# Chunk 0 of a fused attention and FFN kernel: the value projection before q and k, with x and wv loaded side by side

## The chip, the cores and the metric

The kernel runs on one NeuronCore of a Trainium2 chip. The metric is the device time of one execution in microseconds (us), lower is better. Six runs of the kernel before gave a median of 273.89 us, from 273.71 to 274.6.

The core has a matrix engine (TensorE, PE in the profile; its weight loads are PEld), which multiplies a stationary and a moving operand from the on-chip memory SBUF and writes to eight accumulator banks (PSUM); a vector engine (VectorE, DVE), a scalar engine (ScalarE, ACT), GpSimd (POOL), and SyncE (SP). DMA transfers are started by an instruction on SP's or ACT's queue and carried by 16 DMA engines. Engines run on their own and wait for each other on semaphores. Each engine takes its instructions in order.

## What is computed

An input x of 2048 tokens by 512 goes through two branches, which a gate mixes token by token:

```
g = sigmoid((x * gate_w).sum(-1))
a = A(x)                       # attention in 4 segments with a carried memory
b = (relu_gate * up) @ W_down  # FFN: gate = x @ W_gate, up = x @ W_up, F = 1792
out = g * a + (1 - g) * b
```

In A there are 32 heads of 16. q, k and v are x @ wq, x @ wk and x @ wv (512 x 512 each). For each segment of 512 tokens, causal softmax attention within the segment is mixed with a read of a memory matrix M, built from phi(k) and v of the segments before; then comes a projection with wo. All tensors are bf16.

## The kernel before

The kernel is written for four chunks of 512 tokens (NSEG = 4), each of them a segment of the attention. For each chunk there are the projections (`proj`), scores, exponentials and the product with v (`att`, L666), the memory update (`mu`) and its read (`nd`), the FFN (`ffn`, L739), and the output projection (`outp`, L763). A matmul has up to 512 columns; a projection of one chunk is 16 matmuls of 128x512 for each of q, k and v: four output tiles with four contraction tiles (kt) each. q and k come out transposed, four tiles of 128 features by 512 tokens (L581, weights stationary); v comes out by tokens, four tiles of 128 tokens by 512 features (L579, x stationary). So a tile of q or k needs x of all 512 tokens, and a tile of v needs x of its own 128 tokens and all four tiles of wv.

**Who sets the order.** `program` does not write instructions directly. It makes operations (`Op`) that name their engine, an assumed cost and the resources they read and write, and puts them into queues with a priority for each engine (`sc.queue`). A planner (`Sched.run`) then simulates the engines: whenever an engine is free, it takes the head of the queue with the best priority among the heads that are ready by its cost model, and adds the semaphore waits that the resources ask for. The result is a fixed order of instructions for each engine. One queue's operations never overtake each other. TensorE's queues are, by priority: the start (`xps`, 0) and scores (0), memory (1), projections (2), gate matmuls and output (3), FFN (4). An accumulator bank is taken by an `Epoch` when its first matmul is planned, and comes free when its readers are planned; the class "proj" may hold two at once by the planner's account. The planner assumes that DMAs move 340 bytes per ns one after another and land 1.7 us later at the start of the kernel.

**The start.** Loads of 128 KB each go out on two queues (L416 to L421). SP has x row tiles 0 and 2 (into the buffer hT), wq tiles 0 and 2, wk 0 to 3, wv 0 to 3, then beta, the FFN weights wg and wu in halves, the transposed x of chunk 1, gwb, wo and wd (L435 to L441). ACT has x tiles 1 and 3, wq 1 and 3, and gate_w (g4, 1 KB). DVE clears a 128x128 buffer (L473) and the four accumulators. TensorE then works through `xps`: five matmuls of 512 columns on the cleared buffer (`warm(5, 0, 3)`, L482), whose result nobody reads; for each of the four x tiles, four matmuls with the identity, which transpose it into one PSUM bank (L490); and four more of the unread matmuls (`warm(4, 1, 0)`). DVE copies the transposed tiles 0 and 2 to xT, ACT tiles 1 and 3 (L496, L498), 512 columns each. Then the projections begin: q0 and q1 alternate by contraction tile, one matmul for each semaphore wait (L574, L610), then q2, q3, k0 to k3 and v0 to v3 in steps of two matmuls (L609). DVE copies each finished tile out (L588, L594, L607), and masks k per head parity (`kmask`, L597); score matmuls (L679) follow when the first of these is done, exponentials on ACT (L684). The gate's small matmuls (L514, L527) turn gate_w and need g4.

`xt(0)` names the resources of chunk 0's transposed x, one for each row tile; every projection matmul of chunk 0 waits for all four.

The softmax here doesn't subtract the row's maximum and nothing guards it: scores larger than these inputs give would overflow.

## Time and profile before

| | us |
|---|---|
| median of six runs | 273.89 |
| lowest and highest | 273.71, 274.6 |
| the profiled execution | 274.6 |
| its span, first to last instruction | 272.8 |
| TensorE busy in the span | 267.7 |
| VectorE, ScalarE, GpSimd busy | 206.0, 192.8, 123.2 |
| first transposing matmul (L490) starts | 3.29 |
| first projection matmul (L581) starts | 6.99 |

The profile follows one execution. It lists every instruction with its start and duration by engine, and groups them by source line. A duration of a matmul is from its start to the end of its way through the array, and such durations overlap: matmuls in a row start closer together than they last. For a wait it names the instruction or transfer that ended it. "The chain" follows the last instruction back, at each step to what released it. A DMA has the time of its issue, which is an instruction on a queue, and of its landing, when the last of its 16 completion counts arrives; a busy share or a rate of DMA is over all 16 engines. In views by stretches, columns are time busy on each engine with the number of instructions, TensorE's granted clock, DMA share and GB/s.

### The profile page before, as it was taken

What the parts mean: (1) busy time and instruction counts of PE and PEld (TensorE: products, weight loads), DVE (VectorE), ACT (ScalarE), POOL (GpSimd) and SP (SyncE); (2) the same over time, 40 slices, a digit from 0 to 9 for tenths busy, and PEclk for the clock granted to TensorE, in tenths of its full rate; (3) what the DMA queues carried; (4) which work ended last, traced back from release to release, by engine and by line L of the source; (5) the groups of instructions that cost most, each with busy time, mean ns of one, the idle gap of its engine ahead of it and who ended that gap; (6) DMA issues with size and microseconds to landing.
All of it is one profiled execution on the core that took longest, in us unless ns stands there. A gap on an engine that the chain in (4) does not pass through costs nothing.

```text
span 272.8 us, 5368 instructions
## 1 busy us (share of the span) xinstructions
PE 267.7 (98%) x2156; PEld 115.0 (42%) x2156; DVE 206.0 (76%) x421; ACT 192.8 (71%) x182; POOL 123.2 (45%) x171
## 2 busy tenths in 40 slices
PE   6999999999999999999999999999999999999996
PEld 3444434344434544344344444344444343444445
DVE  5689989999989998999978949596774256787200
ACT  3289887788696877889578769985866768782122
POOL 4013566628585676847385663242233343331000
PEclk9999999999999999999999999999999999999999
DMA  6999654011001323120112111000111100000011
GB/s 226 304 348 251 199 87 102 13 40 41 20 2 40 79 58 79 38 48 13 22 38 61 38 42 35 21 2 0 23 37 22 38 23 19 0 2 1 0 41 38
DMA packets 31026, 17.01 MB, mean 62 GB/s; under 512 B 20761, under 2 KB 31001, under 8 KB 31001
## 3 DMA queue, kind: packets, MB, share of 16 engines
q1 hardware_dynamic: 30416, 16.14, 23.3%
q10 hardware_dynamic: 584, 0.53, 0.6%
q8 instruction: 17, 0.28, 0.4%
q14 instruction: 9, 0.07, 0.1%
HBM read 9.84 MB, written 2.10 MB: 44 GB/s over the span
## 4 chain that ended last, share of the span: by engine, by line
PE 93%; DVE 3%; DMA 2%; ACT 1%; issue 0%; SPq 0%; DVEq 0%
PE psA L749 36%; PE psA L788 18%; PE psA L581 10%; PE psL L679 9%; PE psA L704 7%; PE psA L579 5%; PE psA L781 5%; DMA wq<-in_A_wq_dram 2%; PE psA L654 1%; PE psA L625 1%; DVE gexpT L546 1%; ACT E L684 1%; PE psA L641 1%; DVE hT L760 1%; SPq L414 0%
## 5 line engine op out<-in xcount | busy, mean ns | idle before, releaser
L684 ACT ACTIVATE E<-psL 128x2048 bf16<-128x2048 f32 x80 | 150.0, 1875 | 39.4 <-PE psL L679 38.8
L687 POOL TENSOR_SCALAR_AFFINE_SELECT E<-E 128x512 bf16<-128x512 bf16 x128 | 83.1, 667 | 116.3 <-ACT E L684 113.3
L749 PE MATMUL psA<-xT,wu 128*128 128x512 bf16 x224 | 59.8, 380 | 0.0
L749 PE MATMUL psA<-xT,wg 128*128 128x512 bf16 x224 | 59.5, 380 | 0.1
L788 PE MATMUL psA<-wd,hT 128*128 128x512 bf16 (+1 forms) x238 | 54.6, 367 | 0.0
L760 DVE TENSOR_TENSOR hT<-psA,rl 128x512 bf16<-128x512 f32 x56 | 38.3, 683 | 14.0 <-PE psA L749 13.1
L788 PEld LDWEIGHTS psA<-wd,hT 128*128 128x128 bf16 x238 | 21.7, 98 | 24.3 <-issue 3.7
L597 POOL TENSOR_SCALAR kp<-kT,pm 128x512 bf16<-128x512 bf16 x19 | 30.7, 1620 | 2.6 <-PE psL L679 1.2
L679 PE MATMUL psL<-qT,kp 32*128 32x384 bf16 (+3 forms) x512 | 31.7, 301 | 0.0
L749 PEld LDWEIGHTS psA<-xT,wu 128*128 128x128 bf16 x224 | 20.4, 98 | 25.4 <-issue 3.3
L749 PEld LDWEIGHTS psA<-xT,wg 128*128 128x128 bf16 x224 | 20.0, 98 | 24.6 <-issue 3.7
L709 DVE STREAM_TRANSPOSE Tn<-psA 128x512 f32<-128x512 f32 x32 | 21.5, 697 | 8.0 <-PE psA L704 7.9
L757 ACT ACTIVATE rl<-psA 128x512 bf16<-128x512 f32 x28 | 16.7, 597 | 12.7 <-PE psA L749 12.5
L679 PEld LDWEIGHTS psL<-qT,kp 32*128 32x128 bf16 x512 | 8.9, 92 | 31.7 <-ACT E L684 14.4
L758 DVE TENSOR_SCALAR rl<-psA 128x512 bf16<-128x512 f32 x28 | 19.0, 680 | 3.6 <-PE psA L749 2.9
L704 PE MATMUL psA<-E,vaug 128*17 128x256 bf16 (+3 forms) x512 | 21.1, 300 | 0.0
L581 PE MATMUL psA<-xT,wq 128*128 128x512 bf16 x64 | 16.5, 380 | 1.3 <-DMA wq<-in_A_wq_dram 1.3
L781 PE MATMUL psA<-wo,oT 128*128 128x512 bf16 (+1 forms) x68 | 16.5, 367 | 0.0
L581 PE MATMUL psA<-xT,wk 128*128 128x512 bf16 x64 | 16.4, 381 | 0.0
L797 DVE TENSOR_SCALAR osb<-psA,omg 128x512 bf16<-128x512 f32 x8 | 6.0, 746 | 12.9 <-PE psA L788 12.9
L579 PE MATMUL psA<-wv,xT 128*128 128x512 bf16 x64 | 15.7, 380 | 0.0
L798 ACT ACTIVATE osb<-psA,omg 128x512 bf16<-128x512 f32 (+1 forms) x9 | 5.8, 639 | 13.7 <-PE psA L781 13.3
(75 smaller groups left out, 235.6 us busy)
## 6 DMA issues: line engine op xcount, KB each, us to landing
out_dram<-osb SPq DMA_DIRECT2D x15, 128.0 KB, 1.7
wg<-in_B_W_gate_dram SPq DMA_DIRECT2D x8, 224.0 KB, 5.2
wu<-in_B_W_up_dram SPq DMA_DIRECT2D x8, 224.0 KB, 5.8
wd<-in_B_W_down_dram SPq DMA_DIRECT2D x1, 1792.0 KB
osb<-in_A_x_dram SPq DMA_DIRECT2D x12, 128.0 KB, 2.2
wk<-in_A_wk_dram SPq DMA_DIRECT2D x4, 128.0 KB, 5.2
wv<-in_A_wv_dram SPq DMA_DIRECT2D x4, 128.0 KB, 4.7
wo<-in_A_wo_dram SPq DMA_DIRECT2D x1, 512.0 KB, 5.3
```

The lines of the kernel that those rows point to most:

```text
L579: ins = e.matmul(A(ep)[:, :], lhsT=V.xT[:, kt, tok + col * 128:tok + (col + 1) * 128], rhs=w[:, kt, :], start=(kt == 0), stop=(kt == KT - 1))
L581: ins = e.matmul(A(ep)[:, :], lhsT=w[:, kt, col * 128:(col + 1) * 128], rhs=V.xT[:, kt, tok:tok + 512], start=(kt == 0), stop=(kt == KT - 1))
L597: km = lambda e, G=G, p=p, ks=ks: e.tensor_scalar(V.kp[:, ks, :], V.kT[:, G, :], V.pm[:, p:p + 1], None, ALU.mult)
L679: ins = q.matmul(PL[:, jj, o:o + w], lhsT=V.kp[32 * jj:32 * jj + 32, kslot(s, n), 128 * j:128 * j + 128], rhs=V.qT[32 * jj:32 * jj + 32, q ...
L684: acts.append(act(lambda a, e=e: a.activation(V.E[:, e, :, :], PL[:, :, :], ACT.Exp, scale=SCALE), t_act(2048), reads=[f"bankL{b}" for b i ...
L687: pools.append(pool(lambda g, ap=ap: g.affine_select(out=ap, in_=ap, compare_op=ALU.is_ge, fill=0.0, base=0, pattern=[[0, 4], [1, 128]], c ...
L704: ins = q.matmul(A(ep)[32 * jj:32 * jj + 17, c:512], lhsT=V.vaug[:, s % 2, j, 8 * G + 2 * jj + p, :], rhs=V.E[:, e, jj, o:o + w], start=(j ...
L709: ds.append(dve(lambda e, p=p, ep=eps[p]: e.transpose(V.Tn[:, p, :], A(ep)[:, :]), t_dve(512), writes=[f"Tn{p}"], name=f"tr{s}_{G}_{p}", e ...
L749: ins = e.matmul(A(ep)[:, :], lhsT=w[:, kt, f * 128:(f + 1) * 128], rhs=V.xT[:, kt, c * 512:(c + 1) * 512], start=(kt == 0), stop=(kt == K ...
L760: evs.append(dve(lambda e, ep=eu, r=r, hs=hs: e.tensor_tensor(V.hT[:, hs, :], A(ep)[:, :], V.rl[:, r, :], ALU.mult), t_dve(512), reads=[f" ...
L781: ins = e.matmul(A(ep)[:, 0:c1 - c0], lhsT=V.oT[:, o0 + G, i * 128:(i + 1) * 128], rhs=V.wo[:, G, c0:c1], start=st_ and G == 0, stop=sp_ a ...
L788: ins = e.matmul(A(ep)[:, 0:c1 - c0], lhsT=V.hT[:, slots[f], i * 128:(i + 1) * 128], rhs=V.wd[:, f, c0:c1], start=st_ and f == f0, stop=sp ...
```

## The change

The new order of loads pairs each x row tile on SP with the wv tile of the same number on ACT. wq, wk and gate_w follow on SP alone.

The transposes of each x tile are split into two halves of two matmuls, each with a PSUM bank of its own (eight halves take turns in four banks). DVE copies the first half of every tile to xT and ACT the second, 256 columns each, and there is one resource for each half.

The value projection of chunk 0 moves into TensorE's start queue. Its matmuls wait for the wv tiles they use and, alone among the projections, only for the half of the x tile they use. q and k of chunk 0 follow in the order q0, k0, q1, k1 and so on, all in steps of two matmuls; the alternation of q0 and q1 is gone.

The unread matmuls at the start read a constant that the program start writes, in place of the buffer that DVE cleared; there are six instead of five, and the four after the transposes are gone.

```diff
 def xt(c):
-    return [f"xT{c}_{kt}" for kt in range(KT)] if c else [f"xT0_{i}" for i in range(4)]
+    return [f"xT{c}_{kt}" for kt in range(KT)] if c else [f"xT0_{i}_{h}" for i in range(4) for h in range(2)]
...
-for i, eng in enumerate(("sp", "act", "sp", "act")):
-    load(eng, [f"hT{i}"], V.hT[:, i, :], x0[:, i, :], 1 << 17)
-for nm, w, src in (("wq", V.wq, A_wq), ("wk", V.wk, A_wk), ("wv", V.wv, A_wv)):
+for i in range(4):
+    load("sp", [f"hT{i}"], V.hT[:, i, :], x0[:, i, :], 1 << 17)
+    load("act", [f"wv{i}"], V.wv[:, i, :], A_wv[i * 128:(i + 1) * 128, :], 1 << 17)
+for nm, w, src in (("wq", V.wq, A_wq), ("wk", V.wk, A_wk)):
     for kt in range(KT):
-        load("act" if nm == "wq" and kt % 2 else "sp", [f"{nm}{kt}"], w[:, kt, :], src[kt * 128:(kt + 1) * 128, :], 1 << 17)
-load("act", ["g4"], V.g4[:], gate_w.rearrange("(kt p) -> kt p", p=128), 1 << 12)
+        load("sp", [f"{nm}{kt}"], w[:, kt, :], src[kt * 128:(kt + 1) * 128, :], 1 << 17)
+load("sp", ["g4"], V.g4[:], gate_w.rearrange("(kt p) -> kt p", p=128), 1 << 12)
...
-ds.append(dve(lambda e: e.memset(V.rl[:, 0, 0:128], 0.0), 130, writes=["rl0"], name="warm0"))
...
-            ins = e.matmul(PL[:, b, :], lhsT=V.rl[:, 0, 0:128], rhs=V.rl[:, 0, 0:128].unsqueeze(1).to_broadcast([128, 4, 128]), start=True, stop=True)
+            ins = e.matmul(PL[:, b, :], lhsT=nc.const_aps.tensor(1.0, [128, 128], BF16), rhs=nc.const_aps.tensor(1.0, [128, 512], BF16), start=True, stop=True)
...
-xps, xcs = [warm(5, 0, 3)], []
+xps, xcs = [warm(6, 0, 3)], []
 for i in range(4):
...
+    for h in range(2):
+        bk = (2 * i + h) % 4
...
+            for k in range(2):
+                kt = 2 * h + k
+                ins = e.matmul(PL[:, bk, k * 128:(k + 1) * 128], lhsT=V.hT[:, i, kt * 128:(kt + 1) * 128], rhs=V.ident[:], start=True, stop=True)
...
+        if h == 0:
+            xcs.append(dve(lambda e, d=dst, s_=srcp: e.tensor_copy(d, s_), t_dve(256), reads=[f"bankL{bk}"], writes=[f"xT0_{i}_{h}"], name=f"xc{i}_{h}"))
+        else:
+            xcs.append(act(lambda e, d=dst, s_=srcp: e.activation(d, s_, ACT.Copy), t_act(256), reads=[f"bankL{bk}"], writes=[f"xT0_{i}_{h}"], name=f"xc{i}_{h}"))
-xps.append(warm(4, 1, 0))
-sc.queue(0, xps)
...
-        step = 1 if s == 0 and name == "q" and col < 2 else 2
+        step = 2
...
-            pes.append(pe(fn, mm(512, step), reads=[f"{wname}{kt}" for kt in range(k0, k0 + step)] + xt(s), ...
+            pes.append(pe(fn, mm(512, step), reads=[f"{wname}{kt}" for kt in range(k0, k0 + step)] + ([f"xT0_{col}_{k0 // 2}"] if s == 0 and tokmajor else xt(s)), ...
...
     if s == 0:
-        pes = [p for k in "qkv" for p in pes if p.name[0] == k]
-        pes[:2 * KT] = [pes[h * KT + kt] for kt in range(KT) for h in range(2)]
+        vs = [p for p in pes if p.name[0] == "v"]
+        pes = [p for p in pes if p.name[0] != "v"]
+        sc.queue(0, xps[:5] + vs[0:1] + xps[5:7] + vs[1:2] + xps[7:] + vs[2:])
```

In the last line, `xps` holds the unread matmuls, then the halves of row tiles 0 to 3 in order, and `vs` the two halves of v0, v1, v2 and v3.

## The prediction

> **What bounds the kernel now.** I read the page first, for the share of each engine and the chain that ended last; then the busy time by stretches of the span; then TensorE's timeline and the chain within the first 20 us; then the DMA issues one by one and the bytes moved in those microseconds.

> ```profile
> PE 267.7 (98%) x2156; PEld 115.0 (42%) x2156; DVE 206.0 (76%) x421; ACT 192.8 (71%) x182; POOL 123.2 (45%) x171
> ...
> PE 93%; DVE 3%; DMA 2%; ACT 1%; issue 0%; SPq 0%; DVEq 0%
> ```

> TensorE is busy 98% of the span and is 93% of the chain. The stretches show where the other 5.1 us are:

> ```profile
> core 0: us, PE busy (x) PEld busy (x) DVE busy (x) ACT busy (x) POOL busy (x), PEclk, DMA share, GB/s
> ...
> 4.28:7.69 3.41, 2.15 (x17) 1.02 (x15) 1.04 (x2) 1.40 (x3) 0.19 (x1) 1.00 1.04 348
> ...
> 11.10:18.30 7.20, 7.20 (x43) 2.96 (x42) 6.63 (x18) 4.37 (x6) 0.65 (x1) 1.00 1.04 385
> 18.30:260.00 241.70, 241.37 (x2008) 101.81 (x2007) 193.66 (x393) 182.64 (x167) 119.15 (x155) 1.00 0.20 46
> ```

> Between 18.3 and 260 us TensorE misses 0.33 us in all. So nothing downstream can absorb or win back a shift: if the projections of chunk 0 end a microsecond earlier or later, so does the kernel. Only the first 18 us need a sum. TensorE's own timeline there:

> ```profile
> 1.04 2.31 PE L482 MATMUL psL<-rl 128*128 128x512 bf16 x5 [1.04 <-DVE rl L473]
> 3.29 1.52 PE L490 MATMUL psL<-ident,hT 128*128 128x128 bf16 x16
> 4.69 1.04 PE L482 MATMUL psL<-rl 128*128 128x512 bf16 x4
> 6.99 1.89 PE L581 MATMUL psA<-xT,wq 128*128 128x512 bf16 x8 [1.26 <-DMA wq<-in_A_wq_dram]
> ```

> L482 computes nothing that is used. Useful are the 16 transposes (L490) and, from 6.99 on, 48 projection matmuls in a row (16 each of q, k, v), with nothing missing between them. The 6.99 is set by a transfer, as the chain says:

> ```profile
> 1.71 5.19 DMA wq<-in_A_wq_dram
> 6.89 0.09 issue
> 6.99 1.89 PE psA L581 x8
> ```

> **Units.** Eight q matmuls take 1.89 us, the last one 0.38 long: (1.89 - 0.38) / 7 = 0.216 us apart. The last six transposes start 0.056 apart. Before: 6.99 + 48 x 0.216 = 17.36 us for the end of the projections (a gate matmul of 0.11 and the first score matmuls come on top in both kernels).

> **When the data is there.** Each queue issues a 128 KB load about every 0.47 us, so the first eight go out as four pairs, one on SP and one on ACT. Taken one by one, the DMA issues land 2.5 and 2.7 us after issue (pair one, at 3.3 to 3.5 us), 2.7 and 2.9 (pair two, 3.9 to 4.1), 5.2 and 5.4 (pair three, 6.9 to 7.1), 5.4 and 5.6 (pair four, 7.6 to 7.81). Before, pairs one and two are x, three and four are wq. In the new kernel pair n is x row tile n on SP and wv tile n on ACT: the same eight loads in size, the same issue times.

> ```profile
> 2.50:3.50 1.00, 1.00 (x5) 0.21 (x4) 0.70 (x3) 0.19 (x1) 0.86 (x3) 1.00 1.08 370
> 3.50:4.50 1.00, 1.00 (x14) 1.00 (x13) 0.56 (x1) 1.00 (x1) 0.90 (x3) 1.00 0.75 217
> 4.50:5.50 1.00, 1.00 (x10) 0.45 (x7) 0.82 (x2) 0.99 (x3) 0.00 (x0) 1.00 1.05 347
> ```

> The last column is GB/s: full rate, a dip in 3.5 to 4.5, full rate. Of the 16 completion counts of the first wq tile, fifteen are in by 5.54 us and the last at 6.90; of pair four fifteen are in by 6.43 and the last at 7.81: one trailing DMA engine of sixteen holds each load back by some 1.4 us.

> **The change, part by part.**

> *Value projection first.* Each value tile needs all of wv and one x row tile. The new order is: warm-up, transposes of rows 0 and 1, first half of v0, transposes of row 2, second half of v0, transposes of row 3, v1, v2, v3, then q and k. The first half of v0 needs wv0 and wv1 (pair two, 4.1 us) and the first copy of row 0 (transposed from 3.4 us, copied by about 4.3): it runs near 4.4 us in time that is idle or warm-up now. The second half needs wv2 and wv3, so pair four, and TensorE issues in order: until 7.81 it can do only the transposes of row 2 besides. Then come 4 transposes (4 x 0.056 = 0.22) and 46 matmuls (9.94). With the 0.09 from landing to matmul that the chain shows: 7.81 + 0.09 + 0.22 + 9.94 = 18.06, against 17.36: **+0.70 us**. In words: two matmuls (0.43) and nearly all transposes are done under the wait, but the wait now ends with pair four, not pair three, 0.91 us later; q0 and q1 alternate by wq tile today, so two matmuls can start on each tile as it lands.

> Without the trailing engine, the old start is set by the copies of x (the second on ACT ends at 4.60 + 1.09 = 5.69, so 5.8), the new one by pair four at 6.43: 6.43 + 0.09 + 0.22 + 9.94 = 16.68 against 5.80 + 10.37 = 16.17: +0.51. I take **+0.6**, between the two.

> *Copies in halves.* 4 DVE casts of 256 columns instead of 2 of 512 (0.69 us each), and the same on ACT (0.59). The trace has no such cast; bounds are half and all of 0.69; I take 0.47, as the ACT row of 128x256 (0.473) stands to its 512 form (0.69). In total some 0.5 us more on DVE and 0.4 on ACT, which are idle from 5.3 and 5.7 to 8.7 and 9.0 us now. Cover: the copies of row 3 have v1 and v2 (8 x 0.216 = 1.7 us) before v3 asks for them. Uncovered, one copy and its wait, 0.6. Taken at 0. The ACT table load (1.28 us, from 3.31 now) can come one DMA issue earlier, near 2.7.

> *Warm-up.* Six matmuls on a constant instead of five after a DVE memset: they start near 0.8 instead of 1.04, cost 6 x 0.43 = 2.56 us and end near 3.4, where the first x row lands (3.3). Cost 0.1 at most, before a wait that lasts to 7.8: nothing. The four bridging ones go; they fill idle time now, so this gives nothing by itself.

> *Queues.* SP issues 13 loads before beta instead of 12, so beta, wg, wu and the transposed x of chunk 1 go 0.47 us later. wg (issued at 6.9, landing 4.1 later) is first used at 18.8, chunk 1 lands by 23.8 and is used from 26.2: covered. gate_w moves from ACT's fifth place to SP behind wk; it then lands near beta's 10.6 us instead of before its matmul at 8.80. That matmul stands in TensorE's order, and what would queue behind it is all of TensorE; the planner places it after its own estimate of the landing, and TensorE runs later than planned here. Bounds 0 and about 1 us; taken at 0.

> *Order q0, k0, q1, k1.* The same 32 matmuls; wk follows wq on SP and is in by 9.1 us, q starts near 11.2. Score matmuls move; each visit of TensorE to them costs some 0.2 us (from 13.89 + 0.22 to 14.52 around a score group, of which 0.22 is work), over some hundred visits, so a plan with three more or fewer moves the end by 0.6 either way. I take 0, and keep 0.6 both ways.

> **The sum and the median.** The profiled execution took 274.6 us (span 272.8, 1.8 around it) and is the highest of the six; the median is 273.89. With +0.70 the profiled one would take 275.3. The median lies 0.7 lower, which the trailing engine alone could make. On the median: 273.89 + 0.6 = **274.5 us**.

> **The rivals.**

> *A, the forecast: pair four replaces pair three as the last wait.* +0.3 to +0.9, 274.2 to 274.8. For: the landings above. Chance 0.48, of which 0.28 over the bound and 0.20 within it (0.2% of 273.89, 0.55 us, is about what a measurement of this kernel can tell from no change).

> *B, not slower: the first 1.05 MB come faster.* Place: the dip of 3.5 to 4.5 and the trailing engine both begin where wq begins; read together with x from the start, wv may not have them. By bytes: 126 KB by 2.5 us, 370 in the next, then 217, then 347 per us give 1,049 KB at 5.47, and pair two landed 0.5 after its bytes: 5.97. Without the dip, 2.5 + 923 / 370 = 4.99, landing at 5.5. The end of the projections is then 5.97 + 0.09 + 0.22 + 9.94 = 16.22, 1.14 below the profiled 17.36, so 274.6 - 1.14 = 273.5; at 5.5, 273.0. It decides from a landing of pair four before about 7.1 (in the profiled run's terms). Against it: nothing in the rows says that the late engine belongs to wq. Chance 0.27: 0.20 faster, 0.07 within.

> *C, the clock.* TensorE matmuls start 0.427 apart at first and 0.216 from about 4.3 us on; the trace's clock record has full clock from 4.28, 3.24 after the first matmul. Then the old kernel works on to 5.7 and idles 1.26 without losing it. The new one has between 4.3 and 7.9 only about 0.7 us of work. If the clock falls, or comes one period later, 3.2 us of projections run at half rate: +1.6 on A, 276.1. The idle pieces are under 2.1 us each, which no row tests. Chance 0.15, slower.

> [...]

> *D, the order downstream,* by the visits above: 273.9 +- 0.6 around no shift at the start. Chance 0.10, half faster and half slower.

> **The numbers.** Faster 0.20 + 0.05 = 0.25; within 0.20 + 0.07 = 0.27; slower 0.28 + 0.15 + 0.05 = 0.48. The range takes in most of B (273.1) and C to where the clock comes back halfway (275.6); A alone is 274.2 to 274.8.

> **What would show it.** A: TensorE idle for over 1.5 us in all between 4.8 and 8 us, ended by the wv or x load of pair four, and the first L581 (q) matmul near 11.2. B: second half of v0 before 6.5 us, q before 10.2. C: v or q matmuls 0.43 apart. D: more or fewer score visits than now at the same q start. I am wrong if v0 finishes early, or if a stall not named here stands between v3 and the FFN.

## The result, and the profile after

| | before | after |
|---|---|---|
| median, us | 273.95 (37 runs) | 275.05 (17 runs) |
| lowest and highest | 273.55, 274.82 | 274.65, 276.85 |
| the profiled execution | 274.6 | 276.56 |
| its span | 272.8 | 274.8 |

The kernel became slower: the ratio is 1.0056, with a 95% interval of 1.0043 to 1.0069. The forecast of 274.5 had the sign, and its +0.6 is about half of the step between the medians (1.1 us) and two fifths of what the ratio gives (1.53). The range of 273.1 to 275.6 holds the median. The 17 runs after do not lie in one heap: ten are between 274.65 and 275.11 (median 274.97), seven between 276.33 and 276.85 (median 276.55), and none in between. All of the upper seven lie above the range. The profiled execution is one of them.

First the page of the kernel after: busy time by engine, and the shares of the chain that ended last.

```profile
PE 269.3 (98%) x2153; PEld 114.9 (42%) x2153; DVE 205.7 (75%) x414; ACT 197.0 (72%) x196; POOL 117.5 (43%) x167
...
PE 82%; DVE 11%; ACT 3%; DMA 2%; issue 1%; ACTq 0%; DVEq 0%
```

TensorE is still busy 98% of the span, but DVE is now 11% of the chain, where it was 3%. This hints that DVE holds TensorE up somewhere after the start, which the prediction had at nothing; the stretches further down show where. Next TensorE's timeline from the start of the span:

```profile
0.82 2.72 PE L482 MATMUL psL<-const-bfloat16-1.0 128*128 128x512 bf16 x6 [0.82 <-PEq L884]
3.79 1.11 PE L494 MATMUL psL<-ident,hT 128*128 128x128 bf16 x8 [0.25 <-DMA hT<-in_A_x_dram]
4.79 1.01 PE L581 MATMUL psA<-wv,xT 128*128 128x512 bf16 x2
6.05 0.61 PE L494 MATMUL psL<-ident,hT 128*128 128x128 bf16 x4 [0.24 <-DMA hT<-in_A_x_dram]
7.35 1.01 PE L581 MATMUL psA<-wv,xT 128*128 128x512 bf16 x2 [0.69 <-DMA wv<-in_A_wv_dram]
8.15 0.63 PE L494 MATMUL psL<-ident,hT 128*128 128x128 bf16 x4
8.58 3.52 PE L581 MATMUL psA<-wv,xT 128*128 128x512 bf16 x12
11.93 1.03 PE L583 MATMUL psA<-xT,wq 128*128 128x512 bf16 x4
```

Read first the waits: the second half of v0 is held by wv until 7.35, as the forecast had it (pair four). Then the durations: a pair of value matmuls lasts 1.01 us, where the same pair lasts 0.59 in experiment 1 below, so they run at half rate: from 8.58 us on the value matmuls start 0.427 us apart, and from 10.21 on 0.216. The record of the clock has full rate only from 10.115 us. From 7.35 on that concerns six matmuls and four transposes; the seventh value matmul starts at 10.21. They take 2.86 us, and at the prediction's steps 6 x 0.216 + 4 x 0.056 = 1.52 would do: 1.34 lost. q starts at 11.93.

The chain within the first 20 us names the same transfer and the same stretch:

```profile
2.21 5.00 DMA wv<-in_A_wv_dram
7.21 0.14 issue
7.35 1.01 PE psA L581 x2
8.36 0.43 PE psL L494 x4
8.78 3.31 PE psA L581 x12
```

The busy time by stretches, and TensorE's waits by what ended them:

```profile
18.30:260.00 241.70, 240.74 (x2012) 101.07 (x2010) 194.27 (x389) 188.32 (x183) 114.07 (x152) 1.00 0.20 46
```

```profile
PE psL L482 <- PEq L884: 0.8, 1, 0.8
PE psA L581 <- DMA wv<-in_A_wv_dram: 0.7, 1, 0.7
PE psA L581 <- DVE amem L661: 0.5, 1, 0.5
PE psL L494 <- DMA hT<-in_A_x_dram: 0.5, 2, 0.2
PE psA L583 <- DVE amem L661: 0.3, 1, 0.3
```

TensorE misses 0.96 us between 18.3 and 260, where it missed 0.33. Two of these waits are new and have one cause: a projection (v of chunk 2, and k of chunk 3 later) takes the accumulator bank that DVE's scaling of the memory read (L661) has yet to empty. DVE's timeline shows what stands ahead of the first one:

```profile
86.55 0.95 DVE L605 TENSOR_TENSOR ek<-ek,ttmp 128x512 bf16<-128x512 bf16 x1
87.42 0.28 DVE L604 TENSOR_SCALAR ttmp<-kT 128x512 bf16<-128x512 bf16 x1
87.62 1.28 DVE L661 TENSOR_TENSOR amem<-psA,rdm 128x512 bf16<-128x512 f32 x2
```

The two scalings, L661, end at 88.90, and the projection starts at 88.36, when the first of them is done. The change edits nothing there. The planner, given another start, put DVE's work of 87 us in another order.

Against the profile before: the projections of chunk 0 without the work between them end 1.49 us later (18.85 instead of 17.36, 1.34 of it the clock), and from 18.3 to 260 us TensorE misses 0.63 more (0.96 instead of 0.33). That makes 2.1, and the spans differ by 2.0. This is one profile against one, and the experiments show that single profiles do not carry such a sum.

### The profile page after: what moved, and what is told of

Same layout as the page of the kernel before. It is cut to its first block, busy times and chain, and to the rows that moved or that the text cites. A ratio compares the mean times of both kernels' runs of the same rounds, so it can differ in the third digit from the quotient of the medians.

```text
span 274.8 us, 5376 instructions
## 1 busy us (share of the span) xinstructions
PE 269.3 (98%) x2153; PEld 114.9 (42%) x2153; DVE 205.7 (75%) x414; ACT 197.0 (72%) x196; POOL 117.5 (43%) x167
## 4 chain that ended last, share of the span: by engine, by line
PE 82%; DVE 11%; ACT 3%; DMA 2%; issue 1%; ACTq 0%; DVEq 0%
PE psA L752 33%; PE psA L791 15%; PE psA L583 8%; PE psL L682 8%; PE psA L707 6%; PE psA L581 6%; PE psA L784 4%; DMA wv<-in_A_wv_dram 2%; ACT E L687 1%; DVE osb L538 1%; DVE ek L605 1%; DVE hT L763 1%; DVE adT L719 1%; ACT gexpT L549 1%; DVE phiq L594 1%
## 5 line engine op out<-in xcount | busy, mean ns | idle before, releaser
L752 PE MATMUL psA<-xT,wg 128*128 128x512 bf16 x224 | 60.2, 380 | 0.0
L752 PE MATMUL psA<-xT,wu 128*128 128x512 bf16 x224 | 58.8, 380 | 0.0
L763 DVE TENSOR_TENSOR hT<-psA,rl 128x512 bf16<-128x512 f32 x56 | 38.2, 682 | 10.6 <-PE psA L752 9.7
L760 ACT ACTIVATE rl<-psA 128x512 bf16<-128x512 f32 x31 | 18.5, 595 | 13.1 <-PE psA L752 9.2
L599 POOL TENSOR_SCALAR kp<-kT,pm 128x512 bf16<-128x512 bf16 x15 | 24.6, 1640 | 4.3 <-PE psL L682 2.9
L761 DVE TENSOR_SCALAR rl<-psA 128x512 bf16<-128x512 f32 x25 | 17.1, 684 | 4.1 <-PE psA L752 3.8
L581 PE MATMUL psA<-wv,xT 128*128 128x512 bf16 x64 | 17.3, 408 | 1.2 <-DMA wv<-in_A_wv_dram 0.7
L583 PE MATMUL psA<-xT,wk 128*128 128x512 bf16 x64 | 17.0, 380 | 0.3 <-DVE amem L661 0.3
L801 ACT ACTIVATE osb<-psA,omg 128x512 bf16<-128x512 f32 (+1 forms) x11 | 7.1, 647 | 13.7 <-PE psA L784 13.3
L707 PEld LDWEIGHTS psA<-E,vaug 128*17 128x17 bf16 x512 | 10.5, 90 | 10.8 <-issue 3.0
```

What stands on the lines that cost most here:

```text
L581: ins = e.matmul(A(ep)[:, :], lhsT=V.xT[:, kt, tok + col * 128:tok + (col + 1) * 128], rhs=w[:, kt, :], start=(kt == 0), stop=(kt == KT - 1))
L583: ins = e.matmul(A(ep)[:, :], lhsT=w[:, kt, col * 128:(col + 1) * 128], rhs=V.xT[:, kt, tok:tok + 512], start=(kt == 0), stop=(kt == KT - 1))
L599: km = lambda e, G=G, p=p, ks=ks: e.tensor_scalar(V.kp[:, ks, :], V.kT[:, G, :], V.pm[:, p:p + 1], None, ALU.mult)
L707: ins = q.matmul(A(ep)[32 * jj:32 * jj + 17, c:512], lhsT=V.vaug[:, s % 2, j, 8 * G + 2 * jj + p, :], rhs=V.E[:, e, jj, o:o + w], start=(j ...
L752: ins = e.matmul(A(ep)[:, :], lhsT=w[:, kt, f * 128:(f + 1) * 128], rhs=V.xT[:, kt, c * 512:(c + 1) * 512], start=(kt == 0), stop=(kt == K ...
L763: evs.append(dve(lambda e, ep=eu, r=r, hs=hs: e.tensor_tensor(V.hT[:, hs, :], A(ep)[:, :], V.rl[:, r, :], ALU.mult), t_dve(512), reads=[f" ...
```

## The experiments

Three theories were to be told apart: **A**, the wait for pair four; **C**, the clock, which comes late or is lost when TensorE waits there; **D**, the order that the planner makes of the rest. Where a kernel has a fixed order, the planner's choice is replaced by a list:

```diff
+    sc.force = ORDER
     sc.run()
```

Ratios are against the kernel before, run on the same chip (274.07, 273.98 and 274.16 us in the three sessions).

**1. The new kernel with unread matmuls in its gaps.**

```diff
+                if (i, h) == (2, 0):
+                    unread(e, PL[:, bk, :], 1)
                 for k in range(2):
...
+                    if s == 0 and tokmajor and col == 0 and k0 == 0:
+                        unread(e, A(ep)[:, :], 2)
```

> The changed kernel with three unread matmuls in the gaps of its start: two ahead of the first half of v0, one ahead of the transposes of row 2; the order of everything else is the changed kernel's. Theory (late full clock): the runs of the changed kernel fall into two groups 1.5 us apart (near 275.0 and near 276.5) because in some of them TensorE is idle too much for the full clock in the window that ends before the second half of v0, and 8 value matmuls and 4 transposes run at half rate. Then the upper group goes away, all runs lie near 275.0, and the profile shows value matmuls 0.216 apart from the second half of v0 on. Rival (the groups come from the transfers, a DMA engine that trails in some runs): two groups as before, 275.0 and 276.5, and the three extra matmuls add 0 to 0.6.

Median 274.87 us (274.23 to 275.43, one heap), ratio 1.0027 [1.0013, 1.0040]. The heap at 276.5 is gone. The "window" of the theory was a supposition, which no row of this run shows; the record of the clock stands at experiment 3. TensorE's timeline of this kernel, from the same waits on:

```profile
7.24 0.59 PE L589 MATMUL psA<-wv,xT 128*128 128x512 bf16 x2
7.67 0.39 PE L500 MATMUL psL<-ident,hT 128*128 128x128 bf16 x4
7.89 2.75 PE L589 MATMUL psA<-wv,xT 128*128 128x512 bf16 x12
10.48 1.03 PE L591 MATMUL psA<-xT,wq 128*128 128x512 bf16 x4
```

The same two matmuls take 0.59, and q starts 1.45 us earlier. Three matmuls that compute nothing make the kernel faster. The waits on the counterpart of L661 stay (0.5 and 0.3 us).

**2. The old start, then the new order (from 22 us on).**

> The kernel before up to 22 us (its loads, its order of q, k, v and of the first scores), then the instruction order of the changed kernel, written out as a list. Theory (the order downstream has a price of its own: the changed kernel's profile has stalls of 0.69 and 0.44 us at 87 and 120 us, the old one a single one of 0.28): 274.5 to 274.8, that is +0.5 to +0.85 over 273.95, with the stalls at the same instructions. Rival (the whole loss is made at the start, as the prediction has it): 273.95 within 0.2.

Median 275.07 (274.23 to 275.37), ratio 1.0025 [1.0013, 1.0037]. With nothing of the change in the first 22 us, the new order alone costs about 0.7 us, and the two waits are in its profile, on the same instructions, and end at 87.0 and 119.1 us. So the order has a price of its own, which the forecast had at 0.

**3. The new start, then the old order.**

> The counterpart: the changed kernel up to 22 us, then the old order written out as a list. It has two small waits for scores at the joint, near 23 and 26 us, 0.4 and 0.15 us at most. Theory (start and downstream each cost some half of the loss, and the late clock comes on top): lower group 274.2 to 274.8, upper group 1.4 higher, no stall of 0.69 at 87 us. Rival (all of it at the start): 275.0 to 275.5 and 276.5 to 277.

Two heaps again: five runs from 274.10 to 274.98 (median 274.37), seven from 275.86 to 278.21 (median 276.23); over all of them 1.0058 [1.0031, 1.0085]. The new waits downstream are gone; the 0.2 us that the old order always had and a wait of 0.2 for scores at the joint are left, and the heap 1.9 us higher stays. Its profile (276.52 us) was of the upper one, and here the record of the clock shows what happens. By stretches, cut where that record changes (the granted clock is the third column from the right):

```profile
3.90:7.32 3.41, 1.51 (x12) 0.58 (x10) 1.26 (x3) 1.21 (x4) 0.56 (x2) 1.00 0.96 309
7.32:10.73 3.41, 3.27 (x11) 1.44 (x12) 1.11 (x3) 0.61 (x2) 0.00 (x0) 0.50 0.89 255
10.73:14.00 3.27, 3.27 (x16) 1.47 (x15) 2.81 (x7) 0.00 (x0) 0.00 (x0) 1.00 1.02 342
```

Full from 3.904 us, half (0.50) from 7.317, full again from 10.731: steps of 3.413 and 3.414 us. In the first stretch TensorE worked 1.51 us of 3.41, and then the clock was at half for one more such step. Compare the stretch from 4.28 to 7.69 of the kernel before, shown in the prediction, which is as long and held 2.15 us of work, among it the four bridging matmuls: it kept the clock. So the stretch ahead of the loss was not an idle one.

The record of each run also has its mean granted clock, and one half-rate stretch of 3.41 us in 274.8 makes that 0.994. Five of the seven upper runs of the kernel after have 0.994, and none of its lower ten has less than 0.999. Here it is four of the seven upper ones (0.994 to 0.988) and none of the five lower ones (all 1.000). The other upper runs have 1.000, the profiled execution of the kernel after among them: there the clock came late, and as its record begins with the first full clock at 10.115 us, the half rate ahead of that is not counted. So most of the upper runs have a mean that one or two lost stretches make; for the ones with 1.000 that were not profiled, a late clock is not shown. No execution of a lower heap was profiled.

**4. wv loaded after x, value projection still first.** x takes pairs one and two as before, wv three and four, v0 and v1 alternate by wv tile, the bridging matmuls are back; the rest as in the new kernel.

```diff
-    for i in range(4):
-        load("sp", [f"hT{i}"], ...)
-        load("act", [f"wv{i}"], ...)
+    for i, eng in enumerate(("sp", "act", "sp", "act")):
+        load(eng, [f"hT{i}"], ...)
+    for i, eng in enumerate(("sp", "act", "sp", "act")):
+        load(eng, [f"wv{i}"], ...)
...
+    xps.append(warm(4, 1, 0))
...
-            step = 2
+            step = 1 if s == 0 and tokmajor and col < 2 else 2
```

> The changed kernel's value-first order, but with the loads of before: x in pairs one and two, wv in pairs three and four (wq and wk after it), v0 and v1 alternating by wv tile, four unread matmuls after the transposes; all after the value projection in the changed kernel's order. Theory (it is the pairing of x with wv that makes the start wait for pair four and lose the clock, not the value projection): the start is as in the kernel before, no second group, and only the downstream part is left: 274.3 to 274.8. Rival (value first costs by itself, whatever the loads): 275.0 or more.

Median 274.47 (274.14 to 275.02), ratio 1.0012 [1.0001, 1.0024], one heap. v starts at 6.43 and q at 9.88; the two waits downstream are there. Less of a loss than experiment 1 by 0.15% of the time, with the same order behind it; the intervals overlap.

**5. The start of 4, then the old order (from 27 us on).**

> The start of e4 (value first, wv behind x, v0 and v1 alternating) up to 27 us, then the old order. Theory (start and downstream add up: e4 is +0.33 with the new order downstream, which e2 puts at +0.68): the start of e4 alone is 0.3 better than the old one, so 273.6 to 273.8 against 274.0 for the kernel before, unless the joint, where some score matmuls may wait up to 0.6 us, takes it back. Rival (e4's gain comes from how its start fits the new order, not from the start): 274.0 or more.

Median 274.21 (273.79 to 275.27), ratio 1.0010 [0.9996, 1.0023]. The expected gain did not come. The old order behind the better start is worth nothing that can be measured (1.0012 to 1.0010), although the two waits of 0.8 us in all are gone from its profile.

**6. Experiment 3 with the unread matmuls of 1.** The new start with no clock lost and the old order behind it, so mainly the wait for pair four.

> e3 (the changed kernel up to 22 us, then the old order) with the three unread matmuls of e1 in the gaps of its start: the changed start with neither the late clock nor the new order downstream, so what is left is the wait for pair four. The prediction's step A: +0.3 to +0.9, 274.3 to 274.9, in one group. Rival (from e1 less e2: the wait for pair four costs next to nothing against the old start, since that start is itself late in many runs): 273.9 to 274.2.

Median 274.60 (274.06 to 274.86), ratio 1.0022 [1.0011, 1.0034], one heap. The ratio is worth 0.60 us of 273.98, the forecast's +0.6 for A. Its timeline has the long wait, at full clock:

```profile
5.12 0.59 PE L704 MATMUL psA<-wv,xT 128*128 128x512 bf16 x2
6.76 0.39 PE L603 MATMUL psL<-const-bfloat16-1.0 128*128 128x512 bf16 x1 [1.05 <-DMA hT<-in_A_x_dram]
6.99 0.39 PE L615 MATMUL psL<-ident,hT 128*128 128x128 bf16 x4
7.40 0.59 PE L704 MATMUL psA<-wv,xT 128*128 128x512 bf16 x2
```

**7. The kernel before without its four bridging matmuls**, the order of the rest unchanged.

```diff
-    xps.append(warm(4, 1, 0))
```

> The kernel before without its four bridging unread matmuls, everything else in the same order. Theory (the clock needs the gap filled): a second group of runs appears, 0.8 to 1.8 us above, and in a profile of that group the q matmuls start 0.427 apart. Rival (the clock was lost only because of the longer gap in the changed kernel): times as in the kernel before, 274.0, or 0.1 to 0.5 less where the bridging matmuls stood in the way.

Five runs from 273.55 to 274.03 (median 273.9), seven from 275.33 to 276.04 (median 275.53); over all 1.0030 [1.0008, 1.0052]. The old kernel gets the second heap too, 1.6 us up, once nothing fills its wait. In the profile (275.45 us, of the upper heap) q starts 0.91 us earlier than in the profile before and runs at half rate:

```profile
3.50 1.89 PE L605 MATMUL psL<-ident,hT 128*128 128x128 bf16 x16 [0.15 <-DMA hT<-in_A_x_dram]
6.08 3.60 PE L695 MATMUL psA<-xT,wq 128*128 128x512 bf16 x8 [0.69 <-ACT xT L613]
```

Eight matmuls take 3.60 us instead of 1.89. The 16 transposes take 1.89 instead of 1.52, as in the profile of experiment 2, where the four unread matmuls behind them still run at half rate (1.73 us instead of 1.04); so the full clock had probably not come before the wait either. All twelve runs have a mean granted clock of 1.000, so nothing in the record shows a clock that was lost here; in the profile it is not there when q starts. This is C without any of the change. The lower five are as fast as the kernel before, so its bridging matmuls cost nothing that shows when the clock is there anyway.

**8. Experiment 4 with DVE's order mended**, so that neither scaling of the memory read stands behind work that nobody waits for.

```diff
-... mum1_0 gexpT#29 gexpT#31 kphi1_2 kts1_3 ndm1_0 ndm1_1 ...
+... mum1_0 gexpT#29 gexpT#31 ndm1_0 ndm1_1 kphi1_2 kts1_3 ...
...
-... ndc2 gexpT#38 gexpT#39 gexpT#40 ndm2_0 ...
+... ndc2 ndm2_0 gexpT#38 gexpT#39 gexpT#40 ...
```

> e4 with three VectorE instructions drawn forward: the scaling of the first two memory reads of chunk 2 ahead of a phi(k) step, and of the first of chunk 3 ahead of three small gate copies; TensorE's order is e4's. Theory (the two stalls downstream are banks that VectorE gives back late, in the order that the planner drew): the stalls of 0.69 and 0.44 us at 85 and 118 us go, 273.3 to 273.6. Rival (VectorE is late for another reason, or the wait moves to what is queued behind): the stalls stay or come back at the next instruction, 274.2 to 274.5.

Median 274.48 (274.15 to 278.17), ratio 1.0029 [1.0005, 1.0053]; one run of 278.17 makes it wide, the only one of the twelve with a mean clock of 0.994, which explains some 1.7 of its 3.7 us. The median is that of experiment 4. The waits for L661 are gone from the profile, and two others stand in their place:

```profile
PE psA L825 <- DVE kT L714: 0.3, 1, 0.3
PE psA L870 <- DVE qT L708: 0.2, 1, 0.2
```

Until 119.3 us TensorE waits 0.2 us for DVE's copy of q, which stands behind the three gexpT copies that were put back, and elsewhere 0.3 us for that of k. The expected gain of 0.6 to 0.8 us did not come: part of the wait moved.

**9 to 11. The smaller parts of the change, each in the kernel before.** Number 9 has the copies of x in halves (one bank for each tile, as before). Number 10 has the unread matmuls on the constant, six at the start and four after the transposes. Number 11 has both, with two after the transposes.

```diff
-xps, xcs = [warm(5, 0, 3)], []
+xps, xcs = [warm(6, 0, 3)], []
...
-                ins = e.matmul(PL[:, b, :], lhsT=V.rl[:, 0, 0:128], ...)
+                ins = e.matmul(PL[:, b, :], lhsT=nc.const_aps.tensor(1.0, [128, 128], BF16), ...)
```

> The kernel before with the copies of x in halves alone (DVE the first 256 columns of each tile, ACT the second; one bank for each tile, the order of everything else fixed to the order before). The prediction took this part at nothing. Theory: q0 is set by the third pair of loads, not by the copies, so the time stays at the median before, within 0.3 us (273.7 to 274.3); at most the late copy on ACT (5.7 us before) ends some 0.3 earlier. Rival: the two engines hold each other up at a shared bank, or the copies take longer than half (0.42 and 0.38 us in the profile after); then q0 starts later by a copy, 0.4 to 0.6 us, 274.4 to 274.6.

> The kernel before with the unread matmuls on the constant alone, six at the start and four after the transposes, no DVE memset ahead (order fixed). Theory of the clock: what counts is work of TensorE in every 3.4 us period; the matmuls begin 0.22 us earlier (0.82 instead of 1.04) and end near 3.4, so the full clock comes no later than before, and the four after the transposes keep it. Then 273.7 to 274.1, one group of runs. Rival: the sixth one delays the transposes and with them q0, by up to 0.2 us: 274.1 to 274.3.

> The kernel before with halves and the constant together and two unread matmuls after the transposes instead of four (order fixed). Where the full clock comes late, four of them last 1.7 us (one profile has them from 5.37 to 6.93) and stand in front of q0. Theory: with two, q0 starts with the loads, and the clock is still kept: 273.4 to 273.8, faster than before by 0.2 to 0.5 us. Rival: two are too few, and some runs lose a period of clock as in the kernel without any: two groups, the upper one 1.5 us higher (275.2 to 275.8).

| | median, us | lowest, highest | ratio |
|---|---|---|---|
| 9, halves | 274.41 | 273.73, 275.61 | 1.0008 [0.9994, 1.0021] |
| 10, constant | 273.75 | 273.31, 274.50 | 0.9988 [0.9976, 1.0000] |
| 11, both, two bridging | 273.95 | 273.48, 274.25 | 0.9990 [0.9979, 1.0000] |

The halves cost nothing that can be measured. The constant is the one part that may help: 0.12% less, with the end of the interval at no change. Number 11, expected 0.2 to 0.5 us faster, has the same end. None of the three has a second heap (number 9 has a single run at 275.61), so two bridging matmuls were as good as four here. The 3.4 us period in the expectation of number 10 is the step in the record of experiment 3; that the work in it is what counts was a supposition. The timeline of number 10:

```profile
0.82 2.72 PE L596 MATMUL psL<-const-bfloat16-1.0 128*128 128x512 bf16 x6 [0.82 <-PEq L996]
3.35 1.33 PE L604 MATMUL psL<-ident,hT 128*128 128x128 bf16 x16
4.75 1.05 PE L596 MATMUL psL<-const-bfloat16-1.0 128*128 128x512 bf16 x4
5.74 1.90 PE L695 MATMUL psA<-xT,wq 128*128 128x512 bf16 x8
```

These rows have no wait after 0.82 us. q starts at 5.74, just after the last copy of x on ACT (done at 5.68): SP's two wq loads took 3.7 us from issue to landing here (median), while in the profile before they took 5.3, and the first of them landed at 6.90.

## Why the prediction was right or wrong

**The wait (A): right, and near the forecast size.** The last wait is pair four. The new start without a lost clock costs 0.60 us (experiment 6; its interval is worth 0.3 to 0.9); that is the wait together with the halves, the constant and the queues, of which the halves on their own measured 0.08% more and the constant 0.12% less, both with no change inside the interval or at its end (9 and 10). The terms were off in ways that nearly cancel. Pair four landed at 7.21 us, not 7.81; in the profiles of experiments 1, 3 and 6 the second half of v0, which needs it, starts at 7.24, 7.46 and 7.40. And the old start is often earlier than in the profile it was read from: SP's two wq loads took 5.3 us from issue to landing there (median), and 4.1 and 3.7 in the profiles of experiments 2 and 10; and in five other profiles with the old order of loads (2, 7, 9, 10, 11) q0 started at 6.93, 6.08, 6.89, 5.74 and 6.29, not at 6.99. One profile's landing had been taken for the program's. The same holds for "one trailing DMA engine of sixteen": the last completion count of pair four came 1.38 us after the fifteenth in the profile before, and 0.01 us after it in the profile after. So the sign named for A, q near 11.2, was met by neither: q starts at 11.93 in the profile after, at half rate, and at 10.64 in experiment 6. That the size came out is partly luck.

**Faster loads (B): fell.** Pair three still ends late with wv in wq's place (6.00 and 6.21, then 7.01 and 7.21). Pair four of the new pairing landed at 7.21 us, that of the old order at 7.81 in the profile before and by about 7.04 in experiment 10, where the seventh q matmul, which needs it, starts (5.74 + 6 x 0.217): no gain shows.

**The clock (C): the step that failed, in its chance.** The loss and its price stood in the text (+1.6 us); the heaps are 1.59 us apart. That a clock which falls or comes "one period later" is missing for 3.2 us was the author's estimate, which no row of the profile before shows; experiment 3 shows one half-rate stretch, of 3.41 us. But C was given 0.15 and left out of the sum: the row beside it had the old kernel idle for 1.26 us and keep the clock. The row that would have spoken was on the page of the prediction: the old stretch had 2.15 us of work in 3.41, a good part of it bridging matmuls which the change takes out, and the new one by the forecast's own figure about 0.7. Seven runs of 17 pay it, 7/17 x 1.59 = 0.65 us in the mean. Experiment 1 takes it away (1.0056 to 1.0027, 0.8 us), experiment 7 gives it to the old kernel.

**"The four bridging ones go; this gives nothing by itself": wrong.** They were counted as filler of idle time. Without them q runs at half rate in the profile of experiment 7 (eight matmuls in 3.60 us instead of 1.89); in the profile before they are 1.04 of the 2.15 us with which it was kept.

**The order (D): mis-sized, taken at 0.** Its bound of 0.6 either way was nearly right, but the new order behind the old start costs 0.68 us (1.0025). It was looked for in the number of score visits, which is 80 in both profiles; the waits for a bank are what the profile shows.

**The parts may not add.** A costs 0.60 and D behind the old start 0.68; both together, without the clock, 0.74 (experiment 1), not 1.28. Each of these has some 0.35 us of uncertainty either way, so this alone shows little. Experiments 4 and 5 point the same way: behind the start of 4, the old order in place of the new one takes both waits out of the profile, and the time stays (1.0012 to 1.0010); in experiment 8 they shrink to 0.5 us in other places, and the median stays. So behind that start these two waits are not worth their 0.8 us, which would be 0.3%. What the order's 0.7 us in experiment 2 consist of is open, and so is whether, and why, another start hides most of them. If one does, the prediction's "nothing downstream can absorb or win back a shift" falls too.

**Copies in halves, queues:** taken at 0, and 0 within the interval for the halves (9). The other queue places were not tried alone.

**The sum.** Lower heap 274.97 - 273.95 = 1.0, and 0.65 for the clock in the mean: 1.65, against 1.53 by the ratio and 1.1 by the medians, as the median lies in the lower heap. The forecast had 0.6 of it. That the median lies in the range is luck in part: the lower heap has D in it, which the forecast took at 0, and the clock moved the median little only because fewer than half of the runs pay for it.

## What to carry to other kernels

Matmuls that compute nothing may be earning or holding the clock: before you take them out, count TensorE's work in the stretch that they fill (here 1.51 us of 3.41 lost it and 2.15 kept it), not its longest gap, and ask what the first useful matmuls cost at half rate (here eight took 3.60 us instead of 1.89). When a program's times lie in two heaps, profile until you have one of each, and take a landing time from several profiles, since the same two loads took 5.3 us to land in one of them here and 3.7 in another. With a planner, give the edit its old order behind it, and the new order the old start, before you explain the time by the edit.
